# Spectral mixing after linear attention: the weights of two modes in one transfer, their products on row halves

## The chip, the cores and the metric

The kernel runs on one core of a Trainium2 chip. The metric is the device time of one execution in microseconds (us). The kernel before has a median of 425.22 us over four runs (425.04 to 426.35). One execution was profiled; its trace tells when each instruction of each engine ran and when each DMA packet moved.

The core's engines are TensorE (PE in the profile; its weight loads are the row PEld), VectorE (DVE), ScalarE (ACT), GpSimd (POOL) and SyncE (SP). GpSimd and SyncE issue the DMA transfers here, and 16 DMA engines carry them out.

## The reference

The computation has two parts. The first is a linear attention without softmax for 8 batches, 8 heads, 576 rows and a head width of 64:

```python
phi(x) = max(x, exp(x) - 1) + 1          # the ELU feature, plus one
kv  = einsum('bhsd,bhse->bhde', phi(k), v)
z   = sum over s of phi(k)
x   = einsum('bhsd,bhde->bhse', phi(q), kv) / (phi(q) . z + 1e-6)   # then heads side by side: 8 x 576 x 512
```

The second part mixes the first 64 frequencies ("modes") of x along the sequence, each with its own complex 512 x 512 matrix, and adds a channel product:

```python
X  = rfft(x, axis=1)[:, :64]
Yr = Xr @ w_r[m] - Xi @ w_i[m]           # per mode m
Yi = Xr @ w_i[m] + Xi @ w_r[m]
u  = x + irfft(Y, n=576)
out = u + max(u @ w_ch, 0)
```

The weights `w_r` and `w_i` are 64 matrices each of 512 x 512 in 32-bit floats: 134 MB in all, read once. q, k and v are 9.4 MB each, and the output is 9.4 MB.

## The kernel before

**Loads.** Everything large comes through GpSimd's DMA queue, because it is cast on the way: q, k and v to 16-bit floats, the weights to bfloat16. `load(b)` (line 159) brings q, k and v of a batch; a partition holds runs of 9 rows of 64 numbers. q of the first batch comes uncast through SyncE. `w_load(kk, half, ...)` (line 103) brings half a mode: `half` 0 is `w_r[kk]`, 1 is `w_i[kk]`. A tile `w` is 128 partitions by 8 rows by 512 columns. Partition 2p holds rows 8p to 8p+7 of `w_r`, partition 2p+1 the same rows of `w_i`. So a transfer writes every second partition, 64 runs of 16 KB read and 8 KB written. There are four tiles in `wpool` (`W_KEEP`) and six more in `wpre` (`W_PRE`), the latter only until the first ten modes are done. During the attention stage `w_next()` issues single halves between the loads of batches. Later `w_get(kk)` issues a mode's two halves where the program wants a free tile, and GpSimd waits there until TensorE has finished the product that last read this tile. The last half of mode 63 is cut into four pieces (`PIECES`), so that work on it can begin early.

Each GpSimd transfer also tells its landing on one of eight semaphores in turn, and an issue waits until the transfer eight places before it has landed.

**Attention stage.** For each batch: `exps` (ScalarE) and `features` (VectorE) form phi; `turn_q` transposes phi(q) on TensorE and ScalarE copies the result; `sum_kv` sums phi(k) times v; `form_x` divides. `transform` multiplies x with the DFT matrix (`fwd_sb`), and `place_x` spreads the spectrum over the partitions with 0/1 matrices so that partition 2p meets `w_r` and 2p+1 meets `w_i`, with Xi negated where needed. It takes four matmuls per batch and ends in `xt_c`, the stationary operand of all products. This stage's order is written out by hand: `pin` keeps an instruction's place in the program.

**Modes.** `mode_product(kk, ...)` (line 401) takes eight matmuls (line 409), each with 128 rows of contraction and at most 32 columns of `xt_c`; the four column groups of the array hold four of the eight at a time (`tile_position=(0, c)`). VectorE (even modes) or ScalarE (odd) evicts the result, four matmuls with `pick_sb` (line 423) add the four groups and transpose, and every eight modes VectorE copies the collected `yt`. For the first ten modes the instructions are not pinned.

Between a mode's product and its picks stand items from the list `work`, so many per mode as `per_slot` says. For modes 10 to 31 the items compute the attention rows again, in the output's layout (`attention_rows`). For modes 32 to 55 they are the fold stage: for each of 36 tiles of output rows `fold` adds the inverse DFT of the first 32 modes, `turn_x` transposes, `channel_product` multiplies with `w_ch`. For modes 56 to 60 they are `form_z`, `form_y` and `fold_lead`, which prepare modes 32 to 55. `keep_warm` puts extra matmuls without use into the stream; `FILL` says how many per mode.

**Tail.** `last_mode` (line 435) forms mode 63's result. Then the last eight modes are transposed and multiplied with `w_ch`, and `finish` adds everything for pairs of output tiles and stores them through SyncE.

## Time and profile before

| | before |
|---|---|
| median of four runs | 425.22 us |
| profiled execution, its own time | 425.11 us |
| its span (first to last instruction) | 423.3 us |
| TensorE busy | 277.4 us (66%) |
| VectorE busy | 216.2 us (51%) |
| ScalarE busy | 159.2 us (38%) |
| GpSimd busy | 89.5 us (21%) |
| moved by DMA | 93.12 MB written, 220 GB/s mean |
| median time from issue to landing, half a mode (512 KB) | 15.9 us (`w_r`), 17.8 us (`w_i`) |
| mean granted TensorE clock | 0.801 |

The span is cut in 40 slices on the page, where a digit is the busy share in tenths. "PEclk" is the granted TensorE clock as a share of full speed. "DMA" is the packets' recorded time as a share of 16 DMA engines; it can be over 1, since records of packets on one engine may overlap. Sizes and GB/s of a transfer count what is written; a cast load reads twice as much. The chain is followed back from the last instruction: at each step to what released it, or to the instruction before it on its engine.

### The profile page before, as it was taken

How to read it: one execution, taken by the hardware profiler on the slowest of the kernel's cores; microseconds unless marked ns; L12 is line 12 of the kernel's file. 1: busy time of each engine (PE TensorE's matmuls, PEld its weight loads, DVE VectorE, ACT ScalarE, POOL GpSimd, SP SyncE). 2: the span in 40 equal slices, each digit the busy share in tenths (PEclk: the TensorE clock that was granted, in tenths of full speed). 3: DMA queues.
4: the chain of work that ended last, by engine and by line, in shares of the span. 5: the costliest groups of instructions: out<-in, count | busy, mean ns of one | idle time of the engine just before them, and what ended most of it. 6: DMA issues, size and time to landing. Idle time of an engine off the chain costs nothing.

```text
span 423.3 us, 6741 instructions
## 1 busy us (share of the span) xinstructions
PE 277.4 (66%) x2762; PEld 143.6 (34%) x2762; DVE 216.2 (51%) x444; ACT 159.2 (38%) x253; POOL 89.5 (21%) x161
## 2 busy tenths in 40 slices
PE   1358677788248543344433488788777879899992
PEld 0246455565112221111211233343333324374420
DVE  4599688894302463433634443444343434522794
ACT  4688578844121100000000144443433335231782
POOL 4222124222220321212221111211111222120000
PEclk9999688889955555555555578988999999999997
DMA  9999999999999999999999999999999999997697
GB/s 213 207 208 209 209 209 210 217 212 212 221 213 217 216 211 217 216 211 215 218 211 216 216 212 214 218 211 215 218 212 214 218 213 215 216 213 159 236 403 304
DMA packets 27550, 93.12 MB, mean 220 GB/s; under 512 B 3072, under 2 KB 15744, under 8 KB 19264
## 3 DMA queue, kind: packets, MB, share of 16 engines
q0 software_dynamic: 23264, 81.48, 96.1%
q1 hardware_dynamic: 4256, 11.22, 7.2%
q8 instruction: 21, 0.34, 0.3%
q14 instruction: 9, 0.07, 0.0%
HBM read 163.93 MB, written 9.44 MB: 410 GB/s over the span
## 4 chain that ended last, share of the span: by engine, by line
DMA 74%; PE 12%; ACT 3%; issue 3%; DVE 3%; POOL 3%; DVEq 0%; POOLq 0%; ACTq 0%
DMA w<-in_moe_w_i_dram 63%; DMA k<-in_k_dram 7%; DMA pick_sb<-row_pick 4%; PE P L409 3%; PE acc L684 3%; PE acc L723 2%; POOL w L109 2%; ACT ke L191 2%; DVE x L278 1%; ACT qe L191 1%; PE kvp L240 0%; PE qTp L220 0%; ACT qT L227 0%; PE eps L623 0%; POOL k L173 0%
## 5 line engine op out<-in xcount | busy, mean ns | idle before, releaser
L409 PE MATMUL P<-w,xt_c 128*32 128x512 bf16 (+1 forms) x504 | 58.2, 537 | 77.7 <-DMA w<-in_moe_w_i_dram 73.7
L109 POOL DMA_DIRECT2D w<-in_moe_w_r_dram x64 | 33.7, 526 | 216.8 <-PE P L409 193.6
L417 ACT CAST ys<-P 128x512 f16<-128x512 f32 x31 | 18.2, 586 | 125.5 <-PE P L409 121.2
L415 DVE CAST ys<-P 128x512 f16<-128x512 f32 x32 | 22.1, 692 | 73.9 <-PE P L409 59.6
L409 PEld LDWEIGHTS <-xt_c 128*32 128x32 bf16 (+1 forms) x504 | 15.9, 159 | 88.1 <-DMA w<-in_moe_w_i_dram 63.7
L623 PE MATMUL eps<-wch,xTw 128*128 128x512 f16 x144 | 40.8, 411 | 0.0
L109 POOL DMA_DIRECT2D w<-in_moe_w_i_dram x67 | 36.3, 541 | 21.1 <-DMA w<-in_moe_w_i_dram 13.6
L604 DVE TENSOR_TENSOR x_main<-ya,x_main 128x512 f32<-128x512 f32 x32 | 22.0, 691 | 33.0 <-PE ya L600 33.0
L145 PEld LDWEIGHTS <-qT 64*128 64x128 f16 (+1 forms) x640 | 21.1, 125 | 51.1 <-issue 38.5
L631 ACT CAST E<-eps 128x512 f16<-128x512 f32 (+1 forms) x40 | 21.2, 540 | 31.6 <-PE eps L623 31.5
L145 PE MATMUL num<-kv,qT 64*128 64x65 f16 (+1 forms) x320 | 13.7, 212 | 22.9 <-ACT kv L251 11.3
L606 ACT CAST x16w<-x_main 128x512 f16<-128x512 f32 x32 | 19.8, 618 | 23.5 <-DVE x_main L604 17.4
L278 DVE TENSOR_TENSOR x<-num,rd 128x512 f16<-128x512 f32 x32 | 22.1, 692 | 1.1
L220 PE MATMUL qTp<-id,qe 128*128 128x128 f16 x144 | 15.8, 298 | 10.1 <-DVE qe L204 9.5
L191 ACT ACTIVATE qe<-q 128x1152 f16<-128x1152 f16 (+1 forms) x16 | 17.9, 1157 | 9.4 <-DMA q<-in_q_dram 9.4
L423 PE MATMUL yt<-pick_sb,ys 128*128 128x16 f16 x252 | 16.2, 175 | 8.0 <-DVE ys L415 3.1
L423 PEld LDWEIGHTS <-ys 128*128 128x128 f16 x252 | 12.0, 102 | 23.5 <-DVE ys L415 7.8
L191 ACT ACTIVATE ke<-k 128x1152 f16<-128x1152 f16 x16 | 17.7, 1152 | 4.9 <-DMA k<-in_k_dram 3.6
L733 ACT ACTIVATE acc<-acc 128x512 f32<-128x512 f32 x34 | 18.1, 581 | 2.3 <-PE acc L684 1.0
L573 DVE TENSOR_TENSOR x_main<-nw,rd 128x256 f32<-128x256 f32 x32 | 11.5, 416 | 14.0 <-PE nw L145 14.0
L623 PEld LDWEIGHTS <-xTw 128*128 128x128 f16 x144 | 13.2, 104 | 13.3 <-issue 5.6
L220 PEld LDWEIGHTS <-qe 128*128 128x128 f16 x144 | 13.6, 139 | 11.1 <-DVE qe L204 9.9
(108 smaller groups left out, 458.9 us busy)
## 6 DMA issues: line engine op xcount, KB each, us to landing
w<-in_moe_w_r_dram POOLq DMA_DIRECT2D x64, 512.0 KB, 15.9
w<-in_moe_w_i_dram POOLq DMA_DIRECT2D x63, 512.0 KB, 17.8
out_dram<-x_main SPq DMA_DIRECT2D x11, 512.0 KB, 3.7
k<-in_k_dram POOLq DMA_DIRECT2D x8, 576.0 KB, 12.9
v<-in_v_dram POOLq DMA_DIRECT2D x8, 576.0 KB, 14.9
q<-in_q_dram POOLq DMA_DIRECT2D x7, 576.0 KB, 13.0
out_dram<-x_main SPq DMA_DIRECT2D x6, 256.0 KB, 3.4
q<-in_q_dram SPq DMA_DIRECT2D x2, 576.0 KB, 4.5
```

What stands on the lines that cost most here:

```text
L109: nc.gpsimd.dma_start(out=w_in[kk][half::2, dcs], in_=rows_of[:, dcs, :])
L145: mm = nc.tensor.matmul(num[hpo][orow, c0 : c0 + 65], qT[rows, hpp, h2, cols], kv_sb[rows, hpp, h2, :])
L191: pin(nc.scalar.activation(out=ev[:, c], in_=heads(nm, b, c), func=AF.Exp))
L220: nc.tensor.transpose(qT_ps[:, j].rearrange("p t r -> p (t r)"), phi["q", b][:, hpp, j].rearrange("p o d -> p (o d)"), id16,)
L278: nc.vector.tensor_tensor(out=dst.rearrange("p (o c d) -> p o c d", o=2, c=4), in0=nv[:, :, :, 0:64], in1=rden.unsqueeze(3).broadcast_to([ ...
L409: nc.tensor.matmul(P[c : c + n, :], xt_cols(dc, kk, n), w[:, dc, :], start=(dc < NDC), stop=(dc >= NDC), tile_position=(0, c), skip_group_ ...
L415: fixed(nc.vector.tensor_copy(out=st, in_=P))
L423: nc.tensor.matmul(yt_ps[:, ec, kk % 8, :], st[:, ec * 128 : ec * 128 + 128], pick_sb)
L604: pin(nc.vector.tensor_tensor(out=x, in0=acc, in1=x, op=ALU.add))
L606: pin(nc.scalar.copy(out=x16w[t], in_=x))
L623: nc.tensor.matmul(e_ps, xT[:, c, :], wch16[:, c, :], start=(c == 0), stop=(c == NDC - 1))
L631: pin(nc.scalar.copy(out=dst, in_=e_ps[:, cols]))
```

## The change

The weights are loaded by pairs of modes. A tile `w` now has 16 rows of 512 columns per partition and holds two modes: partitions 0 to 63 the even mode of pair p, partitions 64 to 127 the odd one, in both `w_r` on even and `w_i` on odd partitions. One transfer brings `w_r` (or `w_i`) of both modes, as 64 runs of 32 KB read and 16 KB written. There are two tiles of double size in `wpool` and three in `wpre`. The last pair keeps transfers of half a mode, in the old layout, with the same pieces at the end.

A product has 16 matmuls of 64 rows per mode, and those of the two modes of a pair alternate between the row halves (`mode_pair`). Both are evicted, then items of `work`, then the picks of both, then more items, then fillers. All pairs are pinned. `place_x` puts the two modes' spectra on the two partition halves, with 24 matmuls per batch, and the last pair's in the old layout. The columns of the DFT matrix are sorted by even and odd modes for this.

q of batches 1 to 7 is read in runs of 18 rows (4608 bytes) instead of 9, and `turn_q` writes with that stride. The items of `work` are dealt anew over pairs (`share`): attention rows over pairs 5 to 14, with the formation of the row sets (`row_sets`, `row_set`), which stood ahead of the loop, put in after eight of them; the fold stage from the end of pair 15 to that of pair 26; the form stage from the end of pair 27 to that of pair 29. There are 24 fillers instead of 64.

```diff
-    fwd = np.concatenate([np.cos(ang), -np.sin(ang)], axis=2)
+    by_parity = np.concatenate([m[0::2], m[1::2]])
+    fwd = np.concatenate([np.cos(ang)[:, :, by_parity], -np.sin(ang)[:, :, by_parity]], axis=2)
...
-    NDW = 2 * NDC
-    XDC = 2 * B * NM
+    NDW = 4 * NDC
+    NDL = NDW // 2
+    NMP = NM // 2
+    XDC = 2 * B * NMP
...
-        c0 = dc * XDC + kk
-        return xt_c[:, c0 : c0 + (n - 1) * NM + 1 : NM]
+        if kk // 2 == LAST:
+            part, dc = slice(0, 128), (dc // NDC * 2 + kk % 2) * NDC + dc % NDC
+        else:
+            part = HALVES[kk % 2]
+        c0 = dc * XDC + kk // 2
+        return xt_c[part, c0 : c0 + (n - 1) * NMP + 1 : NMP]
...
-    W_KEEP = 4
+    W_KEEP = 2
+    pin = tc.keep_in_program_order
     PIECES = (slice(0, 4), slice(4, 6), slice(6, 7), slice(7, 8))
-
-    def w_load(kk: int, half: int, pool, tag: str, bufs: int):
+    HALVES = [slice(0, 64), slice(64, 128)]
+
+    LAST = NM // 2 - 1
+
+    def w_load(p: int, half: int, pool, tag: str, bufs: int):
         if half == 0:
-            w_in[kk] = pool.tile([128, NDW, D], BF16, tag=tag, bufs=bufs, name=f"w{kk}")
-        rows_of = (moe_w_r, moe_w_i)[half][kk].rearrange("(p dc) e -> p dc e", dc=NDW)
-        for dcs in PIECES if (kk, half) == (NM - 1, 1) else (slice(0, NDW),):
-            tc.keep_in_program_order(
-                nc.gpsimd.dma_start(out=w_in[kk][half::2, dcs], in_=rows_of[:, dcs, :])
-            )
+            w_in[p] = pool.tile([128, NDW, D], BF16, tag=tag, bufs=bufs, name=f"w{p}")
+        two = (moe_w_r, moe_w_i)[half][2 * p : 2 * p + 2]
+        pin(
+            nc.gpsimd.dma_start(
+                out=w_in[p][half::2], in_=two.rearrange("g (r dc) e -> (g r) dc e", dc=NDW)
+            )
+        )
+
+    def w_load_last(pool, tag: str, bufs: int):
+        w_in[LAST] = pool.tile([128, NDW, D], BF16, tag=tag, bufs=bufs, name=f"w{LAST}")
+        for g in range(2):
+            for half in range(2):
+                rows_in = (moe_w_r, moe_w_i)[half][NM - 2 + g].rearrange("(p dc) e -> p dc e", dc=NDL)
+                for dcs in PIECES if (g, half) == (1, 1) else (slice(0, NDL),):
+                    dst = w_in[LAST][half::2, g * NDL + dcs.start : g * NDL + dcs.stop]
+                    pin(nc.gpsimd.dma_start(out=dst, in_=rows_in[:, dcs, :]))
 
     w_in: dict[int, object] = {}
 
 
-    W_PRE = 6
+    W_PRE = 3
...
-                "(hp r j) d -> r hp (j d)", r=128, j=NJ
+                "(hp r j) d -> r hp (j d)", r=128, j=2 * NJ if nm == "q" else NJ
...
-                    pin(nc.sync.dma_start(out=t, in_=rows_in[:, c::2, :]))
+                    pin(nc.sync.dma_start(out=t, in_=rows_in[:, :, c * NJ * Dh : (c + 1) * NJ * Dh]))
...
-            t = sA.tile([128, NHP, NJ * Dh], F16, tag=f"{nm}16", bufs=2, name=f"{nm}16_{b}")
+            shape = [128, 2, 2 * NJ * Dh] if nm == "q" else [128, NHP, NJ * Dh]
+            t = sA.tile(shape, F16, tag=f"{nm}16", bufs=2, name=f"{nm}16_{b}")
...
-    def turn_q(b, hpp):
-        qT = q_view(qT_all[b])
-        qT_ps = psA.tile([128, NJ, 2, NP], F16, tag="big", bufs=3, name=f"qTp{b}_{hpp}")
+    def turn_q(b, c):
+        qT = qT_all[b].rearrange("p (x j) -> p x j", j=2 * NJ)
+        qT_ps = psA.tile([128, NJ, 128], F16, tag="big", bufs=3, name=f"qTp{b}_{c}")
         for j in range(NJ):
             pin(
                 nc.tensor.transpose(
-                    qT_ps[:, j].rearrange("p t r -> p (t r)"),
-                    phi["q", b][:, hpp, j].rearrange("p o d -> p (o d)"),
+                    qT_ps[:, j],
+                    phi["q", b][:, c, j].rearrange("p o d -> p (o d)"),
                     id16,
                 )
             )
         pin(
             nc.scalar.copy(
-                out=qT[:, hpp].rearrange("p t (r j) -> p t r j", j=NJ),
-                in_=qT_ps.rearrange("p j t r -> p t r j"),
+                out=qT[:, :, c * NJ : (c + 1) * NJ], in_=qT_ps.rearrange("p j x -> p x j")
             )
         )
 
...
-    place = sA.tile([128, 2, 2, 128], BF16, name="place")
+    place = sA.tile([128, 4, 66], BF16, name="place")
+    place_l = sA.tile([128, 2, 130], BF16, name="place_l")
     nc.vector.memset(place, 0.0)
+    nc.vector.memset(place_l, 0.0)
 
     def make_place():
+        for i in range(4):
+            pin(nc.vector.tensor_copy(out=place[:, i, 1:65:2], in_=id16[:, i::4]))
         for i in range(2):
-            for o in range(2):
-                pin(nc.vector.tensor_copy(out=place[:, i, o, o::2], in_=id16[:, i::2]))
+            pin(nc.vector.tensor_copy(out=place_l[:, i, 1:129:2], in_=id16[:, i::2]))
 
     xsp = {}
+    PARTS = ((0, slice(1, 3)), (1, slice(0, 2)))
 
     def place_x(b):
 
-        x = xsp.pop(b)
-        ps = psA.tile([128, 2, 512], F32, tag="big", bufs=3, name=f"xp{b}")
+        x = xsp.pop(b).rearrange("p t c m -> p c t m")
+        ps = psA.tile([128, 4, NDC, 2, NMP], F32, tag="big", bufs=3, name=f"xp{b}")
+        for i in range(4):
+            for o, ts in PARTS:
+                for g in range(2):
+                    pin(
+                        nc.tensor.matmul(
+                            ps[HALVES[g], i, :, :, 0 : NMP - 1],
+                            place[:, i, 1 - o : 65 - o],
+                            x[:, :, ts, g * NMP : g * NMP + NMP - 1],
+                            start=(o == 0), stop=(o == 1), skip_group_check=True,
+                        )
+                    )
         for i in range(2):
-            for o, ts in ((0, slice(1, 3)), (1, slice(0, 2))):
-                pin(
-                    nc.tensor.matmul(
-                        ps[:, i], place[:, i, o, :], x[:, ts].rearrange("p t c m -> p (t c m)"),
-                        start=(o == 0), stop=(o == 1),
+            for g in range(2):
+                for o, ts in PARTS:
+                    pin(
+                        nc.tensor.matmul(
+                            ps[:, 2 * i + g, :, :, NMP - 1],
+                            place_l[:, i, 1 - o : 129 - o],
+                            x[:, :, ts, g * NMP + NMP - 1],
+                            start=(o == 0), stop=(o == 1), skip_group_check=True,
+                        )
                     )
-                )
...
+        h = NDW // 2
+        psf = ps.rearrange("p i c t m -> p (i c) t m")
+        pin(nc.vector.tensor_copy(out=xt_v[:, 0:h, :, b, :], in_=psf[:, 0:h]))
+        pin(nc.scalar.copy(out=xt_v[:, h:NDW, :, b, :], in_=psf[:, h:NDW]))
...
-            if b >= 1:
+            if b % 2 == 1:
...
-    def w_get(kk: int):
-        if kk not in w_in:
+    def w_get(p: int):
+        if p not in w_in and p == LAST:
+            w_load_last(wpool, "w", W_KEEP)
+        elif p not in w_in:
             for half in range(2):
-                w_load(kk, half, wpool, "w", W_KEEP)
-        return w_in.pop(kk)
+                w_load(p, half, wpool, "w", W_KEEP)
+        return w_in[p]
 
...
+    slots: dict = {}
+
+    def work_slot(p: int, name: str):
+        for _ in range(slots.get((p, name), 0)):
+            if work:
+                work.pop(0)()
+
+    def product(P, kk: int, w, dc: int):
+        last = kk // 2 == LAST
+        n_dc = NDL if last else NDW
+        c = dc % NDC * 32
+        n = 32 if dc < NDC else 2 * B
+        rows = slice(0, 128) if last else HALVES[kk % 2]
+        pin(
+            nc.tensor.matmul(
+                P[c : c + n, :], xt_cols(dc, kk, n), w[rows, dc, :],
+                start=(dc < NDC), stop=(dc >= n_dc - NDC), tile_position=(rows.start, c),
+                skip_group_check=True,
+            )
+        )
+
+    def evacuate(kk: int, P):
+        st = ystage.tile([128, D], F16, tag="ystage", bufs=2, name=f"ys{kk}")
         if kk % 2 == 0:
-            fixed(nc.vector.tensor_copy(out=st, in_=P))
+            pin(nc.vector.tensor_copy(out=st, in_=P))
         else:
-            fixed(nc.scalar.copy(out=st, in_=P))
-        work_slot(kk, 0)
-        work_slot(kk, 1)
-        keep_warm(fill[0])
+            pin(nc.scalar.copy(out=st, in_=P))
+        return st
+
+    def picks(kk: int, st):
         for ec in range(NDC):
-            fixed(
+            pin(
                 nc.tensor.matmul(
                     yt_ps[:, ec, kk % 8, :], st[:, ec * 128 : ec * 128 + 128], pick_sb
                 )
             )
...
+
+    def mode_pair(p: int):
+        nonlocal yt_ps
+        w = w_get(p)
+        kks = (2 * p, 2 * p + 1)
+        if p % 4 == 0:
+            yt_ps = psW.tile([128, NDC, 8, 2 * B], F32, tag="yt", bufs=1, name=f"yt{p // 4}")
+        Ps = [psW.tile([128, D], F32, tag="P", bufs=2, name=f"P{kk}") for kk in kks]
+        for dc in range(NDW):
+            for P, kk in zip(Ps, kks):
+                product(P, kk, w, dc)
+        sts = [evacuate(kk, P) for P, kk in zip(Ps, kks)]
+        work_slot(p, "mid")
+        for kk, st in zip(kks, sts):
+            picks(kk, st)
+        if p % 4 == 3:
+            if kks[1] < NF:
+                pin(nc.vector.tensor_copy(out=YE_T[:, :, kks[1] - 7 : kks[1] + 1, :], in_=yt_ps))
+            else:
+                g = (kks[1] - NF) // NL + 1
+                pin(nc.vector.tensor_copy(out=YL[:, :, :, g, :], in_=mode_rows(yt_ps)))
+        work_slot(p, "end")
+        keep_warm(FILL.get(p, 0))
+
+    def last_pair():
+        w = w_get(LAST)
+        kk = NM - 2
+        P = psW.tile([128, D], F32, tag="P", bufs=2, name=f"P{kk}")
+        for dc in range(NDL):
+            product(P, kk, w, dc)
+        st = evacuate(kk, P)
+        keep_warm(4)
+        picks(kk, st)
+        pin(nc.vector.tensor_copy(out=Y8[:, :, 0 : NL - 1, :], in_=yt_ps[:, :, 0 : NL - 1, :]))
+        keep_warm(6)
         kk = NM - 1
-        w = w_get(kk)
-        y_last = ps.tile([128, NDC, 2 * B], F32, tag="P", bufs=2, name="y_last")
-        for dc in range(NDW):
+        y_last = psW.tile([128, NDC, 2 * B], F32, tag="P", bufs=2, name="y_last")
+        for dc in range(NDL):
             for ec in range(NDC):
                 pin(
                     nc.tensor.matmul(
-                        y_last[:, ec, :], w[:, dc, ec * 128 : ec * 128 + 128], xt_cols(dc, kk, 2 * B),
-                        start=(dc == 0 and ec == 0), stop=(dc == NDW - 1), skip_group_check=True,
+                        y_last[:, ec, :], w[:, NDL + dc, ec * 128 : ec * 128 + 128],
+                        xt_cols(dc, kk, 2 * B),
+                        start=(dc == 0 and ec == 0), stop=(dc == NDL - 1), skip_group_check=True,
                     )
                 )
         nc.vector.tensor_copy(out=Y8[:, :, NL - 1, :], in_=y_last)
...
+    FILL = {**{p: 1 for p in range(20, 27)}, 27: 1, 28: 1, 29: 2, 30: 3}
...
+    for p in range(n_early):
+        mode_pair(p)
...
+    sel = sW.tile([128, 1 + N_LEAD, 128], F16, tag="rows", bufs=1, name="row_sel")
+
+    def row_sets():
+        pin(nc.vector.memset(sel, 0.0))
...
+    def row_set(i: int):
+        dst = ([inv2_sb] + lead_sb)[i]
         for cols in (slice(0, 512), slice(512, S)):
             r_ps = bank(f"rows{i}_{cols.start}")[:, 0 : cols.stop - cols.start]
-            nc.tensor.matmul(r_ps, sel[:, i, :], inv_sb[:, cols])
-            nc.scalar.copy(out=dst[:, cols], in_=r_ps)
+            pin(nc.tensor.matmul(r_ps, sel[:, i, :], inv_sb[:, cols]))
+            pin(nc.scalar.copy(out=dst[:, cols], in_=r_ps))
...
+    first_fold, first_form, n_form_p = NF // 2 - 1, NE // 2 - 1, 3
+    fold_pairs = first_form - first_fold
+
...
+    share(
+        n_fold,
+        [((first_fold, "end"), 5)]
+        + [((p, h), 3) for p in range(first_fold + 1, first_form) for h in ("mid", "end")],
+    )
+    share(
+        n_form,
+        [((first_form, "end"), 6)]
+        + [((p, h), 4) for p in range(first_form + 1, first_form + n_form_p) for h in ("mid", "end")],
+    )
...
+    rows_work = [row_sets] + [lambda i=i: row_set(i) for i in range(1 + N_LEAD)]
+    work[:0] = [lambda t=t: attention_rows(t) for t in tiles[:8]] + rows_work + [
+        lambda t=t: attention_rows(t) for t in tiles[8:]
+    ]
+    share(
+        len(tiles) + len(rows_work),
+        [((p, h), 1) for p in range(n_early, first_fold) for h in ("mid", "end")],
+    )
+
+    for p in range(n_early, LAST):
+        if p == LAST - 1:
...
+            slots[p, "mid"] = slots[p, "end"] = N_PRE
...
+        mode_pair(p)
+    last_pair()
+
+
+    last = sW.tile([128, 2, D], F16, tag="rows", bufs=1, name="last")
```

## The prediction

> **What bounds the kernel now.** I read the page's head and its slices first, then the DMA queues, then the stage table, then the chain that ended last, then single rows of TensorE.
>
> ```profile
> span 423.3 us, 6741 instructions
> PE 277.4 (66%) x2762; PEld 143.6 (34%) x2762; DVE 216.2 (51%) x444; ACT 159.2 (38%) x253; POOL 89.5 (21%) x161
> ...
> PEclk9999688889955555555555578988999999999997
> DMA  9999999999999999999999999999999999997697
> ...
> q0 software_dynamic: 23264, 81.48, 96.1%
> ```
>
> No compute engine is near full; the DMA row is at 9 in all but two slices. GpSimd's queue (q0) alone has packet time for 96.1% of the span, that is 407 us, though its loads run only from 5.5 to 391.4 us (first packet; last landing). So packets overlap each other, and most of a packet's recorded fixed time is hidden already. The stage table (columns: stretch, its length, then busy time and count of each engine, granted clock, DMA share, GB/s) shows the same:
>
> ```profile
> 24.00:40.00 16.00, 11.82 (x148) 9.50 (x149) 15.16 (x33) 13.18 (x15) 4.04 (x6) 1.00 1.19 210
> 160.00:200.00 40.00, 15.83 (x212) 7.19 (x216) 14.95 (x43) 2.34 (x4) 8.46 (x16) 0.50 1.04 215
> 260.00:290.00 30.00, 23.64 (x166) 10.31 (x164) 12.76 (x25) 12.49 (x24) 7.11 (x14) 0.90 1.03 214
> 390.00:423.30 33.30, 24.70 (x160) 8.91 (x160) 22.99 (x24) 19.73 (x38) 0.56 (x1) 0.93 0.80 301
> ```
>
> The share is 1.19 where packets are short (q, k, v) and 1.03 to 1.04 with weights, at nearly the same GB/s. The chain in order of time (start, us, what):
>
> ```profile
> 250.17 17.83 DMA w<-in_moe_w_i_dram
> 268.05 0.71 PE P L409 x7
> 269.56 17.99 DMA w<-in_moe_w_i_dram
> 287.60 0.72 PE P L409 x6
> 289.12 17.98 DMA w<-in_moe_w_i_dram
> ```
>
> Landings at 268.00, 287.55 and 307.10: 19.55 us for four modes, 4.89 per mode, whatever TensorE does between. A load waits 18 us because some 13 to 15 us of other loads stand ahead of it. Only an empty queue, or fewer bytes or less overhead in it, moves the last landing. Behind that lies a tail of 423.3 - 391.4 = 31.9 us, paced by VectorE (busy 23.0 us of 33.3).
>
> Now TensorE, where the clock is 0.50:
>
> ```profile
> 150.60 1.11 PE L409 MATMUL P<-w,xt_c 128*32 128x512 bf16 x8 [1.66 <-DMA w<-in_moe_w_i_dram]
> 151.65 0.63 PE L145 MATMUL nw<-kv,qT 64*128 64x65 f16 x16
> 152.51 0.28 PE L423 MATMUL yt<-pick_sb,ys 128*128 128x16 f16 x4 [0.23 <-DVE ys L415]
> 155.49 1.10 PE L409 MATMUL P<-w,xt_c 128*32 128x512 bf16 x8 [2.70 <-DMA w<-in_moe_w_i_dram]
> 156.52 0.41 PE L145 MATMUL nw<-kv,qT 64*128 64x65 f16 x8
> ...
> 245.26 0.61 PE L613 MATMUL xTp<-id,x16w 128*128 128x128 f16 x4
> 245.66 1.91 PE L623 MATMUL eps<-wch,xTw 128*128 128x512 f16 x4
> ...
> 249.50 1.03 PE L623 MATMUL eps<-wch,xTw 128*128 128x512 f16 x4
> ```
>
> A product is eight matmuls in two rounds of four column groups: 1.11 us; a record of one round alone took 0.65, so a further round costs 0.46. The 64-row matmuls of L145 alternate row halves: 16 take 0.63, 8 take 0.41, so 27.5 ns each. The last three lines are the fold stage, before and after the clock rose to 1.00 at 247.8.
>
> **Part 1: fewer packets and transfers.** A packet of 1152 B (written) is recorded with 107.2 ns, one of 8192 B with 625.2: 73.6 ns per 1000 B. A q, k or v transfer (32 packets per engine) so needs 32 x 1152 B = 2.71 us and lands every 2.845; a half of a mode (4 packets) needs 2.411 and lands every 2.443. The residues, 0.13 and 0.032 us, give (0.13 - 0.032) / 28 = 3.5 ns per packet and 0.018 us per transfer. The 31 first pairs take 62 transfers instead of 124, and 16 KB packets instead of 8 KB ones: per engine 4 x 62 = 248 packets fewer, 0.87 us, and 62 transfers fewer, 1.12 us. q of batches 1 to 7: 16 packets fewer per engine each, 7 x 16 x 3.5 ns = 0.39 us. Together 2.4 us. No row shows a 32 KB read; if it is cut in two packets, only 1.12 + 0.39 = 1.5 us go. At the other end all the weights' residue cannot go, so 2.4 is also the upper bound. I take 2.4, because the 16 KB read went as one packet.
>
> The Trainium skill, "DMA: Bandwidth & Descriptors", section "Anatomy of one DMA", fits 2.0 us plus bytes per transfer. By that 62 transfers fewer would give an estimated 124 us, if nothing overlapped; the row above has 0.032 us of everything that is not bytes, so the measurement decides.
>
> **Part 2: TensorE instructions.** The products become 1000 matmuls instead of 504, with 64 rows each. If both modes of a pair run side by side, as the halves in L145 do, a pair is four rounds: 0.65 + 3 x 0.46 = 2.03 us at half clock, against 2 x 1.11 = 2.22 before. If one follows the other it is eight rounds, 0.65 + 7 x 0.46 = 3.87. I take 2.03, by the L145 row, which is nearest. `place_x` goes from 4 to 24 matmuls per batch, half as wide or tiny: by 27.5 ns each between 0 and 0.6 us per batch, in a stage where loads stand 8.4 us or more ahead of each issue; nothing on the path. Three more instructions on VectorE (two copies of 0.24, one memset of 0.27), once, lie there too. The q copy, exps and features keep their sizes (1124 to 1157 ns). Row sets move from before the loop into the slots of pair 7: six matmuls (3.1 us) and eleven small VectorE instructions, where TensorE idles half the time. Fillers fall from 64 to 24.
>
> The Trainium skill, "TensorEngine Tiling (Array Packing)", section "Instruction Overhead", counts about 60 cycles of overhead per matmul, which speaks against the change. With the 2.4 GHz of its page "TensorE: Matmul & The Clock Gate" (introductory table) that is an estimated 12 us of TensorE for the 496 added ones. The products' rows above put them beside the transfers, and L145 shows starts 27.5 ns apart, so the sum would not move by it unless a pair's slack were used up.
>
> More code is fetched: 1232 more instruction rows on TensorE, with 21 packets for the present 6741 instructions some 4 packets of 0.95 us on one engine each, 0.24 us over 16; up to 0.95 if they all fall on the slowest. I take 0.25.
>
> **Part 3: cover that shrinks.** Buffers hold the same bytes, but come free by pairs. In the steady state a new load was issued with 13.2 us of landings ahead (three modes less 1.45). Now it is one pair, 9.7 us, less 2.03 for the product and 0.32 to issue: 7.4 us. What does an empty queue need? The tail's GpSimd load was issued at 394.01 with its first packet at 395.98, and a landing is told 0.33 us after the last packet: 2.3 us. So 5 us of lateness are free. Places:
>
> - Pairs 1 to 5. `pick_sb` landed at 125.30, and is now 0.7 earlier, 124.6. Then picks, product, eviction, picks of each pair follow in a fixed order: 2.03 + 0.8 (product's end to pick, as at 151.7 to 152.5) + 0.3 = 3.13 us. Product 5 ends at 124.95 + 4 x 3.13 + 2.03 = 139.5; pair 7 is issued at 139.85. Pair 6 lands at 124.6 + 19.4 = 144.0: 4.15 us are left, 1.85 above the need. Price 0; this is the thinnest place.
> - Fold stage (end of pair 15 to 26). A tile (fold, transposition, channel product) takes about 2.8 us at half clock and 1.5 at full, by the starts of these rows; three tiles and one transposition of 0.6 per pair are 9.0 or 5.1 us, plus product 2.03 or 1.15 and picks 0.4. That is 6.7 of 9.7 us at full clock; an all-cold pair needs 11.4 and makes the next 1.7 late, where 5 are free. Price 0.
> - Pair 29's product waits for form work of pair 28: about 1.6 us late, price 0. The last pair keeps the old transfers, pieces and `y_last`, and the tail its order; 0.
>
> **Sum.** -2.4 + 0.25 = -2.15 us: span 421.15. The profiled execution took 425.11, 1.81 over its span and 0.11 under the median of 425.22. So 422.96 for an execution like it and 423.07 against the median; I say 423.0. A difference of 0.3%, 1.3 us, is about what a measurement can tell from no change.
>
> **Rivals.**
> - The 32 KB run goes as two packets: 425.2 - 1.5 + 0.25 = 424.0, within 0.3%. For it: no row with 32 KB. Against: a packet already equals the whole 16 KB run.
> - Slower: the two row halves don't run side by side with four column groups each. From 0.4 us more per pair on, pairs 1 to 5 (1.85 / 5) let the queue run dry; at the full 1.84 us, product 5 ends 9.2 us later, and pair 7 is issued at 149.05 with its first packet at 151.0, when data ended at 143.7: 7.3 us of empty queue, 423.0 + 7.3 = 430.3. With half the loss, 2.7 us: 425.7. For it: no row of before uses row halves and 32-column groups at once. Against: each of the two is seen to overlap on its own.
> - Fold or form stage late by more than 5 us in a pair, with the clock falling to 0.5 since fillers go: each microsecond beyond counts; three pairs with 1 to 2 us are 427 to 429. Against: a busy TensorE got 1.00 at 247.8 without fillers.
> - The stream gains, but the clock falls before `y_last`: 1.61 us of y_last and some 3 us behind it slow, 1 to 1.5 us given back: 424.3.
>
> **How the numbers follow.** Forecast 0.61, two packets 0.07, halves one after another 0.12 (a third with so small a loss that it ends near 426, the rest to 430.3), late fold or form 0.11, cold end 0.09. Faster than 423.9: the forecast and a little of the second, 0.62. Within 0.3%: 0.06 of the second, 0.04 of the third, 0.06 of the cold end, 0.16. Slower than 426.5: 0.08 of the third, the late stages' 0.11 and 0.03 where a cold end goes with them, 0.22. The range starts at 421.8 (both bounds, a tail 1 us shorter by the slots' new order) and reaches to 428.5, which leaves out the worst of the stalls, about 0.1.
>
> **What would show it.** Right: packets of 16 KB, one per run; landings of a pair every 9.70 us instead of 9.77 from 160 to 370 us; the DMA row at 9; products of 32 matmuls in about 2.0 us at clock 0.50; last landing near 389.2 and a tail of 31.9. Wrong: packets of 8 KB; a landing interval near 140 to 155 us well over 5 us; products of 3.9 us; a chain that goes through folds instead of weights; a clock of 0.5 at the end.

## The result, and the profile after

| | before | after |
|---|---|---|
| median of all timed runs (55 and 34) | 425.21 us | 424.98 us |
| profiled execution, its own time | 425.11 us | 425.54 us |
| its span | 423.3 us | 423.7 us |
| last landing of weights | 391.39 us | 390.97 us |
| from there to the end (tail) | 31.9 us | 32.8 us |
| mean granted TensorE clock | 0.801 | 0.750 |

After to before, mean against mean, is 0.9977, with a 95% interval of 0.9969 to 0.9985: 1.0 us faster (0.6 to 1.3), where 2.2 were forecast (423.0). That lies within the 0.3% to which the prediction gave 0.16. Repeated runs of one kernel fall in two groups (before 425.0 to 425.6 and, 20 of 55, 426.2 to 428.1; after 423.5 to 424.0 and, 20 of 34, 424.9 to 425.6), so that the medians differ by only 0.2 us where the means differ by 1.0, and the profiled run of before is of its faster group, that of after of its slower one.

The page of after, its head, slices and DMA queues:

```profile
span 423.7 us, 7890 instructions
PE 283.2 (67%) x3378; PEld 152.2 (36%) x3378; DVE 215.5 (51%) x447; ACT 161.6 (38%) x253; POOL 56.6 (13%) x99
...
PEclk9999978898555555555555587889698896579998
DMA  9999999999999999999999999999999999987697
...
q0 software_dynamic: 16512, 81.47, 93.9%
...
q8 instruction: 26, 0.43, 0.4%
```

Its stage table (stretch, length, busy time and count of each engine, clock, DMA share, GB/s):

```profile
160.00:200.00 40.00, 17.79 (x308) 8.92 (x305) 17.04 (x52) 3.71 (x9) 4.23 (x8) 0.50 1.02 216
260.00:290.00 30.00, 24.48 (x226) 11.25 (x224) 13.85 (x27) 13.15 (x24) 3.17 (x6) 0.89 1.01 215
390.00:423.70 33.70, 25.12 (x166) 9.07 (x163) 23.45 (x25) 19.73 (x38) 0.57 (x1) 0.95 0.78 297
```

q0 has 6752 packets fewer, and its share fell from 96.1 to 93.9% at the same bytes. In the slices, compare the clock: before it stood at 9 from the 29th digit on; now there is a second valley (6, 5, 7) late in the modes, and the DMA row leaves 9 one slice earlier. q8 carries code: 26 packets against 21 before. In the stage table the share is down to 1.02 and 1.01 at much the same GB/s. The chain in order of time shows the steady part:

```profile
174.41 1.94 PE P L442 x25
176.35 0.35 PE nw L165 x8
...
176.72 0.52 POOL w L119
177.23 16.55 DMA w<-in_moe_w_i_dram
...
193.82 1.94 PE P L442 x20
```

Products start 19.41 us apart, here for two pairs (the chain skips every second one): 9.705 us per pair against 9.77 before. A product of 32 matmuls takes 1.94 us at half clock. Pair 30 landed at 379.27, mode 61 of before at 381.49: at that point the stream was 2.22 us ahead. Twelve microseconds later, at the last landing, it was 0.42 ahead, and the tail gave 0.8 back. So in this run the forecast gain existed and was lost behind 379 us. The late part of TensorE in after (start, us, engine, line, what; lines in between are left out):

```profile
371.36 1.98 PE L698 MATMUL z<-wch,YL 128*64 128x512 f16 x8
375.87 1.10 PE L442 MATMUL P<-w,xt_c 64*32 64x512 bf16 x32
383.92 1.10 PE L442 MATMUL P<-w,xt_c 64*32 64x512 bf16 x32
388.08 0.67 PE L442 MATMUL P<-w,xt_c 128*32 128x512 bf16 x8
390.95 1.07 PE L504 MATMUL y_last<-xt_c,w 128*128 128x16 bf16 x32
```

`y_last` in the kernel before, waiting for its weights:

```profile
390.11 1.61 PE L444 MATMUL y_last<-xt_c,w 128*128 128x16 bf16 x32 [0.19 <-DMA w<-in_moe_w_i_dram]
```

And GpSimd's issues in after, with the idle time before them in brackets:

```profile
362.79 0.54 POOL L119 DMA_DIRECT2D w<-in_moe_w_i_dram  x1
377.34 0.52 POOL L131 DMA_DIRECT2D w<-in_moe_w_r_dram  x1 [14.01 <-PE P L442]
```

Pair 29's product began at 375.87, 6.3 us after its weights (369.57). GpSimd waited 14.01 us for it and issued the last pair's loads with 1.92 us of landings ahead. The landings that followed, with their distance to the one before (from the trace's issues and times to landing; 2.44 is the distance in an undisturbed stream):

```
379.27  w_i of pair 30
382.44  +3.17   w_r of mode 62   (late issue: 0.73 over)
384.86  +2.42   w_i of mode 62
388.57  +3.71   w_r of mode 63   (1.27 over; issued with 6.47 us ahead)
390.97          last piece of w_i of mode 63
```

The second jump is not explained by a late issue. A code packet of q8 started at 386.4 us; runs below show what it did.

### The profile page after: what moved, and what is told of

The parts are those of the page before. It is cut to its first block, busy times and chain, and to the rows that moved or that the text cites. A ratio compares the mean times of both kernels' runs of the same rounds, so it can differ in the third digit from the quotient of the medians.

```text
span 423.7 us, 7890 instructions
## 1 busy us (share of the span) xinstructions
PE 283.2 (67%) x3378; PEld 152.2 (36%) x3378; DVE 215.5 (51%) x447; ACT 161.6 (38%) x253; POOL 56.6 (13%) x99
## 3 DMA queue, kind: packets, MB, share of 16 engines
q0 software_dynamic: 16512, 81.47, 93.9%
## 4 chain that ended last, share of the span: by engine, by line
DMA 63%; PE 23%; DVE 4%; ACT 3%; issue 3%; POOL 2%; DVEq 0%; POOLq 0%; ACTq 0%
DMA w<-in_moe_w_i_dram 47%; PE P L442 8%; DMA pick_sb<-row_pick 8%; DMA k<-in_k_dram 7%; PE acc L735 3%; PE z L698 2%; PE acc L774 2%; ACT ke L213 2%; POOL w L119 1%; PE zl L425 1%; DVE ys L452 1%; PE yp L711 1%; PE yt L460 1%; DVE x L299 1%; ACT qT L249 1%
## 5 line engine op out<-in xcount | busy, mean ns | idle before, releaser
L442 PE MATMUL P<-w,xt_c 64*32 64x512 bf16 (+2 forms) x1000 | 53.2, 558 | 61.5 <-DMA w<-in_moe_w_i_dram 60.1
L119 POOL DMA_DIRECT2D w<-in_moe_w_r_dram x31 | 16.5, 533 | 245.2 <-PE P L442 141.0
L442 PEld LDWEIGHTS <-xt_c 64*32 64x32 bf16 (+2 forms) x1000 | 17.1, 128 | 80.0 <-DMA w<-in_moe_w_i_dram 42.8
L676 PE MATMUL eps<-wch,xTw 128*128 128x512 f16 x144 | 43.2, 430 | 0.0
L165 PEld LDWEIGHTS <-qT 64*128 64x128 f16 (+1 forms) x640 | 23.3, 124 | 49.1 <-issue 28.1
L165 PE MATMUL nw<-kv,qT 64*128 64x65 f16 (+1 forms) x320 | 19.0, 240 | 9.5 <-DVE x_tail L620 4.3
L460 PE MATMUL yt<-pick_sb,ys 128*128 128x16 f16 x252 | 11.8, 174 | 14.3 <-DMA pick_sb<-row_pick 7.6
L249 ACT COPY qT<-qTp 128x1152 f16<-128x1152 f16 x16 | 19.6, 1290 | 0.5 <-PE qTp L242 0.2
L460 PEld LDWEIGHTS <-ys 128*128 128x128 f16 x252 | 9.8, 103 | 24.6 <-DVE ys L452 15.3
L119 POOL DMA_DIRECT2D w<-in_moe_w_i_dram x31 | 16.9, 544 | 4.6 <-DMA q<-in_q_dram 2.3
```

The lines of the kernel that those rows point to most:

```text
L119: nc.gpsimd.dma_start(out=w_in[p][half::2], in_=two.rearrange("g (r dc) e -> (g r) dc e", dc=NDW))
L165: mm = nc.tensor.matmul(num[hpo][orow, c0 : c0 + 65], qT[rows, hpp, h2, cols], kv_sb[rows, hpp, h2, :])
L249: nc.scalar.copy(out=qT[:, :, c * NJ : (c + 1) * NJ], in_=qT_ps.rearrange("p j x -> p x j"))
L442: nc.tensor.matmul(P[c : c + n, :], xt_cols(dc, kk, n), w[rows, dc, :], start=(dc < NDC), stop=(dc >= n_dc - NDC), tile_position=(rows.sta ...
L460: nc.tensor.matmul(yt_ps[:, ec, kk % 8, :], st[:, ec * 128 : ec * 128 + 128], pick_sb)
L676: nc.tensor.matmul(e_ps, xT[:, c, :], wch16[:, c, :], start=(c == 0), stop=(c == NDC - 1))
```

## Experiments

Theory at the start: the clock falls to 0.50 in pair 27, so the form stage is slow, pair 29's product late and the queue short. Rivals: the stream gains less than thought, or the form work dealt into pair 28 is too much at any clock.

**Is the stream's gain what it was taken for?** Each transfer of a pair cut in two:

```diff
-out=w_in[p][half::2], in_=two.rearrange("g (r dc) e -> (g r) dc e", dc=NDW)
+runs = two.rearrange("g (r dc) e -> (g r) dc e", dc=NDW)
+for dcs in (slice(0, NDL), slice(NDL, NDW)):
+    pin(nc.gpsimd.dma_start(out=w_in[p][half::2, dcs], in_=runs[:, dcs]))
```

> The changed kernel with each transfer of a pair cut in two of eight rows (124 transfers and 16 KB read per packet as in the kernel before; tiles, products and order stay). Prediction's price (0.018 us per transfer and 3.5 ns per packet): a pair lands every 9.77 us instead of 9.71, pair 30 lands at 381.2 to 381.4 us instead of 379.3, and since pair 29's product waits for the same chain of work after pair 28's landing, the end moves by the same: median 426.5 to 427. If the pair layout itself and not the longer runs made the stream faster, pair 30 still lands at 379.3 and the median stays at 425.0.

Pair 30 landed at 381.25 us, 1.98 later than in after; by 3.5 ns for 248 packets per engine and 0.018 us for 62 transfers it should be 1.98. Median 426.46 us (425.58 to 427.21), at the edge of the expected range; ratio to before 1.0014 (1.0001 to 1.0028).

Then the number of transfers left alone and only the runs halved, by a gap of two numbers in the tile's layout (28 of the 31 pairs):

```diff
-t = pool.tile([128, NDW, D], ...)
+t = pool.tile([128, 2, NDL * D + 2], ...)        # halves no longer adjacent
-in_=two.rearrange("g (r dc) e -> (g r) dc e", dc=NDW)
+in_=two.rearrange("g (r h dc) e -> (g r) h (dc e)", h=2, dc=NDL)
```

> The changed kernel with a gap of two numbers between the two halves of eight rows in the tiles of wpool (pairs 0, 1 and 5 to 30), so that the number of transfers stays and only the runs are cut to 16 KB read. Prediction's price of 3.5 ns per packet: a pair lands every 9.74 us instead of 9.71, that is 28 pairs x 8 packets x 3.5 ns = 0.8 us, pair 30 lands at about 380.0 us. If the whole residue is per transfer, 379.3; if it is all per packet, 381.1.

Pair 30 landed at 379.96, 0.69 later; 224 packets at 3.5 ns are 0.78. One run, 426.25 us. Both prices of the first part stand, each to about 0.2 us, since pair 30 of after itself landed 0.25 us earlier in two later profiles; the rival of a weaker stream falls.

**Does the clock make pair 29 late?** Fillers only:

```diff
-FILL = {**{p: 1 for p in range(20, 27)}, 27: 1, 28: 1, 29: 2, 30: 3}
+FILL = {**{p: 6 for p in range(20, 28)}, 28: 1, 29: 2, 30: 3}
```

> The changed kernel with six fillers per pair from pair 20 to 27 instead of one (the work, the transfers and their order unchanged). Clock theory: the form stage ran at a granted clock of 0.50 (351.8 to 375.7 us) because the idle time of each pair now lies in one piece and has one filler; with the fillers the clock stays at 1.00 from about 325 us on, pair 29's product starts at 369.5 to 371.5 us instead of 375.9, the last loads are issued with 5 us or more of landings ahead instead of 1.9, the last landing comes at about 389.1 instead of 391.0, and the median is 423.0 to 423.4 us. Block theory (two double tiles and form work dealt in big blocks make pair 29 late whatever the clock): the clock rises, but pair 29's product starts after 374 us, the queue still runs dry, and the median stays at 424.5 to 425.

Median 424.73 (423.44 to 426.16), ratio 0.9981 (0.9965 to 0.9998); 423.0 to 423.4 were expected. The profiled run took 423.46 us, one of the two fastest of twelve. The clock was not at 1.00 throughout, as the theory had it, but at 0.50 from 355.3 to 362.2 us; from there to the tail it stayed at 1.00. Its form work and product on TensorE:

```profile
369.68 1.09 PE L698 MATMUL z<-wch,YL 128*64 128x512 f16 x8
...
371.03 1.10 PE L442 MATMUL P<-w,xt_c 64*32 64x512 bf16 x32
```

GpSimd's issue after it:

```profile
372.49 0.52 POOL L131 DMA_DIRECT2D w<-in_moe_w_r_dram  x1 [8.76 <-PE P L442]
```

Eight `z` matmuls take 1.09 us instead of 1.98, the product starts 4.8 us earlier, the loads have 8.04 us ahead, and the tail is 31.9. So the clock decides whether pair 29 is late. But the last landing was 389.75, not 389.1: pair 30 landed 6.23 us after the landing before it instead of 4.85, of which the next landing gave 0.64 back. Something else cost 0.7 us, and the median moved little.

The other way to an early pair 29, less form work in pair 28 (weight 2 instead of 4 in its two slots, 6 in those of pair 29) and the fillers of after:

```diff
-+ [((p, h), 4) for p in range(first_form + 1, ...) for h in ("mid", "end")],
++ [((p, h), 2 if p == first_form + 1 else 6) for p in range(first_form + 1, ...) ...],
```

> The changed kernel with the form work dealt otherwise: weight 2 instead of 4 in the two slots of pair 28, 6 instead of 4 in those of pair 29; fillers as they are. Block theory: pair 29's product starts at 368 to 371 us, the queue never runs dry, last landing near 389.1, median 423.0 to 423.5. Clock theory: the loads are in time as well, but the form work at clock 0.50 is only pushed behind pair 29, so that pair 30's product and mode 62 come late, y_last starts at 391 us or later although its weights landed at 389, and the median is 424.3 to 425.2.

Pair 29's product began at 369.44 and the loads had 8.25 us ahead. The landing behind the issue was not late (381.58: +2.42), yet the median was 426.35 (424.49 to 427.01), ratio 1.0012 (0.9997 to 1.0026), more than either side had expected; the profiled run took 425.76. The work had only moved, as its rows on TensorE show:

```profile
384.30 1.10 PE L442 MATMUL P<-w,xt_c 64*32 64x512 bf16 x32
388.47 0.67 PE L442 MATMUL P<-w,xt_c 128*32 128x512 bf16 x8
391.34 1.07 PE L504 MATMUL y_last<-xt_c,w 128*128 128x16 bf16 x32
```

Pair 30's product stood 5.1 us behind its weights (379.16) and `y_last` ended 2.3 us after the last landing (before: 0.33). At half clock the form work is too long in either place. And a later landing was late by 1.2 us (388.83).

More fillers: sixteen in pair 27, eight of them inside its waits.

```diff
+FILL_27 = 4      # after pair 27's evictions, and again after its picks
-FILL = {**{p: 1 for p in range(20, 27)}, 27: 1, 28: 1, 29: 2, 30: 3}
+FILL = {**{p: 6 for p in range(20, 27)}, 27: 8, 28: 1, 29: 2, 30: 3}
```

> Theory (the gain is lost because the clock falls before the form stage): six fillers in pairs 20 to 26 and sixteen in pair 27, eight of them inside its waits for evictions and copies, keep the granted clock at 1.00 from 345 to 385 us more often than e1_fill's six did. Pair 29's product then begins at 369.5 to 371.5 us, the last loads are issued with over 6 us of landings ahead, the last landing is at 389.1 to 389.8, and the median is 423.0 to 423.7, with fewer than a third of the runs above 424.4 (e1_fill: 9 of 12). Rival (the size of the form stage's pieces is what is late, whatever the clock): no better than e1_fill, 424.7, or worse by the fillers' own time, up to 425.5.

The clock's part held: 1.00 from 340 to 370 and 0.98 to 380, product at 369.43, 9.03 us ahead. The median did not: 424.40 (424.10 to 425.39) where 423.0 to 423.7 were expected, ratio 0.9973 (0.9956 to 0.9989), the same as that of after. Six of twelve runs were above 424.4, and in e1_fill it was eight, not nine as the expectation says. The last landing was 389.75 as in e1_fill, again behind one landing 1.0 us late (379.92).

Whether fewer fillers alone bring the clock down, asked of the kernel before:

```diff
-FILL = {**{kk: (0, 3) for kk in range(44, 60)}, 60: (0, 1), 61: (2, 3), 62: (4, 6)}
+FILL = {**{kk: (0, kk % 2) for kk in range(40, 60)}, 60: (0, 1), 61: (1, 3), 62: (4, 6)}
```

> The kernel before, with its fillers cut from 64 to 24 and nothing else. Theory: fewer fillers let the clock fall to 0.50 somewhere between 295 and 375 us, but with four tiles of one mode each the form work holds up no load long enough: 13 us of landings lie ahead of an issue and 2.3 are needed, so the last landing stays at 391.4 (within 0.3) and the time at 425.2 to 425.9. Rival A (the fillers alone explain the loss): the same half clock costs here what it cost in the changed kernel, 1.5 to 2 us, 426.7 to 427.2. Rival B (the clock falls because of the longer pauses between pairs, not for want of fillers): the clock stays at 1.00 from 295 to 385 and the time at 425.2.

Two windows of after (columns as in the stage table; the clock is third from the end):

```profile
350.00:360.00 10.00, 6.34 (x69) 2.93 (x68) 4.29 (x7) 1.17 (x2) 1.05 (x2) 0.59 0.99 211
360.00:370.00 10.00, 9.48 (x66) 3.15 (x66) 3.19 (x5) 2.39 (x5) 1.06 (x2) 0.50 1.02 218
```

The first of them in the kernel before, with its 64 fillers:

```profile
350.00:360.00 10.00, 9.18 (x76) 4.63 (x75) 4.32 (x8) 4.91 (x9) 2.12 (x4) 1.00 1.04 216
```

Both in the kernel with fewer fillers:

```profile
350.00:360.00 10.00, 8.24 (x59) 4.26 (x60) 3.00 (x6) 3.89 (x7) 1.81 (x4) 0.83 1.03 215
360.00:370.00 10.00, 8.72 (x69) 3.85 (x65) 6.65 (x11) 3.51 (x6) 2.42 (x5) 1.00 1.03 215
```

With 25 fillers (the expectation counts 24) the clock of the kernel before halved for a third of one stretch and came back at once; the last landing was 391.13 and the profiled run took 424.98 us. The median was 425.83, the ratio 1.001 (0.9987 to 1.0033). In the profiled run the theory held, with a shorter fall than it had in mind, and few fillers alone did not keep the clock down as they did in after, where waits are gathered at pairs. But five of the ten runs took 426.4 to 428.1 us and none of these was profiled, so rival A is not ruled out for them.

**Two more profiles of after**, to see what makes its times differ:

> The changed kernel once more, for one more profile. Theory: its times fall in two groups (423.5 to 424.0 and 424.9 to 425.6) by whether the clock is kept. A run under 424.2 shows the clock at 1.00 for most of 345 to 376 us, pair 29's product begun before 373 and the last landing by 389.9; a run over 424.7 shows 0.50 there, the product at 375 to 377 and the last loads issued with under 2.3 us of landings ahead. Rival: the groups differ in the stream itself; pair 30 lands 1 to 1.5 us earlier in the faster one, at the same clock.

> The same kernel and the same expectation as for e0_again1: by the theory a run under 424.2 us has the clock at 1.00 for most of 345 to 376 us and pair 29's product begun before 373, one over 424.7 has 0.50 there and the product at 375 to 377; by the rival the landing of pair 30 differs by 1 to 1.5 us instead.

Both took 424.9 us and are alike: clock valley, product at 375.3, the first late landing only 0.30 over (2.74), the second 1.14 to 1.18 over (3.58, 3.62). So the theory held for a time over 424.7. A time under 424.2, as 14 of the 34 runs had, was not met, and what is different there stays open; the mean clock, on record for each run, does not tell (0.761 to 0.789 in those 14, 0.750 to 0.780 in the others). The jump behind the code packet near 386 was there again.

**The code packets.** I numbered q8's packets in the traces so far. From the 1st to the 26th of e1_fill TensorE ran 3178 matmuls, 127 for each on average. Behind the 17th a landing is late and stays 0.7 to 1.1 us behind, in the kernel before too (at 327.75 us); behind the 18th to 20th it is late by up to 0.9 us, of which all but 0.3 comes back with the next; behind the 25th 0.7 to 1.3 us stay again. Before has 20 packets ahead of its last landing, after 25. Theory: a packet of 0.94 us delays one DMA engine, and the 25th strikes the engine that is already the latest. First, fewer instructions: two batches' spectra placed by one set of matmuls.

```diff
-def place_x(b):                 # 24 matmuls per batch, 31 columns x 8
+def place_two(b):               # 24 matmuls per two batches, 31 columns x 16
...
-            if b > 1 and jj == 1:
-                place_x(b - 2)
+            if b > 1 and b % 2 == 1 and jj == 1:
+                place_two(b - 3)
```

> The changed kernel with the spectrum of two batches placed at once: 96 matmuls fewer on TensorE, nothing else. Theory (the 25th code packet delays the DMA engine that is already the latest): in the traces a code packet of 16 KB comes every 128 matmuls; the 17th and the 25th were followed by a landing 1.0 to 1.3 us late that was not made up, the others not. Here the 25th should come only after the last weights (after 391 us, against 386.4), the landing that took 3.71 us takes 2.4 to 2.6, the last landing is at 389.0 to 389.9 even if the clock falls and the last loads are issued late as before, and the median is 423.5 to 424.4. Rival (only the late issue costs): the last landing stays at 390.2 to 391.0 and the median at 424.7 to 425.2.

Median 423.37 (422.52 to 425.27), just under the expected range; ratio 0.9946 (0.9927 to 0.9965), against runs of before with a median of 426.17. Against the 425.21 of all its runs it is 1.8 us. The DMA queues from 384 to 389.5 us (packets, MB, share), of after:

```profile
q0 software_dynamic: 402, 1.03, 97.4%
q8 instruction: 1, 0.02, 1.1%
```

And of this kernel, with no packet of q8:

```profile
q0 software_dynamic: 361, 0.72, 69.8%
```

The 25th packet came at 390.7 us. The landing behind 386 took 2.44 us instead of 3.71, and the last one was 389.56, although the clock fell here too (0.65 and 0.67 in the two windows from 350 to 370), pair 29's product began only at 373.79 and the loads had 3.63 us ahead (0.63 lost there, +3.07).

Next, both cures:

```diff
 # place_two as above, FILL_27 as in e6_fill27
+FILL_27 = 4
-FILL = {**{p: 1 for p in range(20, 27)}, 27: 1, 28: 1, 29: 2, 30: 3}
+FILL = {25: 2, 26: 6, 27: 8, 28: 1, 29: 2, 30: 3}
```

> The same, with 34 fillers in place of 24 (two after pair 25, six after 26, sixteen in pair 27, the last pairs as in the changed kernel). Theory: both losses go. Clock at 1.00 for most of 345 to 385 us, pair 29's product begun by 372, the last loads issued with over 6 us of landings ahead, no code packet from 377 to 389, last landing at 388.3 to 389.1, and a median of 422.4 to 423.4. Rival (code packets do not matter, or the later code packet moves to another place among the last loads): the last landing is at 389.7 as in e1_fill and e6_fill27, median 423.4 to 424.7.

Its products on TensorE at the end, with the idle time before them:

```profile
379.20 1.11 PE L451 MATMUL P<-w,xt_c 64*32 64x512 bf16 x32 [1.47 <-DMA w<-in_moe_w_i_dram]
384.03 0.66 PE L451 MATMUL P<-w,xt_c 128*32 128x512 bf16 x8 [0.59 <-DMA w<-in_moe_w_i_dram]
387.86 1.44 PE L515 MATMUL y_last<-xt_c,w 128*128 128x16 bf16 x32 [0.80 <-DMA w<-in_moe_w_i_dram]
```

Every product waits for its weights again, none of the last landings is late by more than 0.1 us, and the last is at 388.96: 2.43 us before that of the kernel before. Five of six runs took 423.2 to 423.5. The profiled one is the sixth, 424.86: the clock fell at 389 (0.66 from 389 to 394), and its tail was 34.0 us instead of 31.9. Median 423.38, ratio 0.9944 (0.9928 to 0.9960): the same as e10_lean, and its expected 422.4 to 423.4 just met. (It has 40 fillers; the expectation counts 34.) These two beat both kernels. The earlier last landing, 388.96 against 389.56 in e10_lean, shows in the profiles and not in the medians.

Last, the number against the place: 256 tiny matmuls, so that each late packet's number is two higher.

```diff
+if 6 <= p < 14:
+    for _ in range(32):
+        pin(nc.tensor.matmul(last_ps[0][:, 0:8], id16, wch16[:, 0, 0:8]))
```

> The changed kernel with 256 tiny matmuls more (8 columns each, 32 after each of pairs 6 to 13, where TensorE has time), so that each later code packet has a number two higher. Theory (the number decides): the 25th comes near 350 to 356 us and a landing behind it is 0.9 to 1.3 us late for good, so that pair 30 lands at 380.0 to 380.7 instead of 379.0 to 379.3; the packet near 386 is now the 27th and the landing behind it takes 2.4 to 2.6 us, not 3.7. The last landing stays within 0.5 of 390.6. Rival (what costs is a code packet among the last loads, whichever it is): pair 30 at 379.0 to 379.4 and again 3.6 us at the landing behind 386.

The 25th packet came at 354.0 and the landing behind it took 6.25 us (the next 4.20, so 0.8 stay); the 27th came at 386.8, and the landing behind it took 2.46, where after had 3.71. The 17th moved likewise: it came at 217.1 instead of 249.3, the landing behind it took 6.27 (the next 4.22), and the one behind the packet at 249.0 took 5.01 where after had 5.92. In this run the number decided, not the place. Pair 30 landed at 379.90, 0.1 short of the expected range. The last landing missed it by more: 392.02, since the landing after the late issue was 1.95 over (4.39) with 1.90 us ahead; after lost only 0.73 with 1.92, and what makes the difference stays open. One run, 426.09 us.

## Why the prediction was right or wrong

**Fewer packets and transfers: right, and so were both prices.** A 32 KB run went as one packet (16384 B written, 1229 ns). The forecast was 2.4 us, 2.15 net of code; measured 2.22 at pair 30 (2.45 in the two later profiles), and e2_cut and e5_runs16 gave back 1.98 and 0.69 when the parts were undone. The 0.39 for q was not measured alone. The rival of two packets fell.

**Products on row halves: right.** 1.94 to 1.95 us at half clock against 2.03 worked out, so both modes run side by side. The rival of halves one after another fell; the time of the 496 added matmuls stayed beside the transfers (1.94 of 9.7 us per pair), but not their code, as said below.

**Pairs 1 to 5: the price of 0 was right.** ScalarE's copy behind `turn_q`, kept at 1124 ns in the prediction, took 1290. `pick_sb` came at 125.99 instead of 124.6, pair 7 was issued at 140.91 instead of 139.85, with 4.30 us ahead (forecast 4.15), and the landing behind it took 4.93 us. The steady distance ahead was 7.3 to 7.4 (forecast 7.4).

**"Pair 29's product waits for form work of pair 28: about 1.6 us late, price 0" is the step that failed first.** It was 6.3 us late (6.1 in the later profiles). The prediction gives no working for the 1.6 and names no clock; e1_fill, at 1.00 from 362 us on, had 1.59, so the figure is one of full clock. The rival "Fold or form stage late by more than 5 us in a pair, with the clock falling to 0.5 since fillers go" described it, at 427 to 429 us, but had 0.11, because a busy TensorE got 1.00 without fillers at 247.8. That row shows how the clock rose there, not how it is kept; and in after it stayed at 0.50 until 375.7 though TensorE was busy for 9.48 of the 10 us from 360 to 370. What took it, in windows of 3.4 us of after (its changes of clock are whole multiples of 3.41 us apart):

```profile
344.90:348.30 3.40, 3.30 (x20) 1.32 (x18) 1.08 (x3) 1.94 (x4) 0.00 (x0) 1.00 1.02 217
348.30:351.75 3.45, 1.12 (x33) 0.63 (x32) 0.38 (x1) 0.72 (x2) 0.08 (x1) 1.00 0.94 199
351.75:355.20 3.45, 2.29 (x20) 1.41 (x22) 1.00 (x2) 0.30 (x1) 0.97 (x2) 0.51 1.02 218
```

TensorE was busy 1.12 of 3.45 us, waiting for weights before pair 27's product and for the eviction behind it, and the clock halved at 351.8. The longest idle piece was 1.88 us. The Trainium skill, "TensorE: Matmul & The Clock Gate", section "Why this matters for your kernels", asks for no idle gap over about 3 us between bursts; here a stretch with no such gap was enough, so the measurement decides. The other six falls of after between 245 and 352 us agree: TensorE was busy for 0.5 to 2.1 of the 3.41 us before each and had not been idle for 3 us at a stretch when the clock fell, while after other such windows, with 1.7 us of work and more, it was kept. So what counts looks like the work in such a window, but no exact limit comes out of these runs.

The price in the profiles: the first late landing, 0.73 us (0.30 in the later ones), and the tail. "the tail its order; 0" failed with it, for TensorE came to `y_last` with work left over: it ended 1.05 us after the last landing instead of 0.33, and the tail is 0.8 longer. The need of 2.3 us ahead of an issue does not decide what is lost: e2_cut had 2.85 and lost 0.06, e10_lean had 3.63 and lost 0.63, while 8 us and more (e1_fill, e3_deal, e6_fill27, e12_both) lost nothing.

**"More code is fetched ... I take 0.25" was the mis-sized term.** It spread 0.95 us per packet over 16 engines, and named 0.95 as the bound if all four fall on the slowest; four on one engine would be 3.8. Five more packets came ahead of the last landing, and one of them, the 25th, cost 1.27 us in the profiled run, up to 1.18 in the later profiles, 0.7 to 1.2 net in e1_fill, e3_deal and e6_fill27. Fewer instructions alone (e10_lean) brought the median from 424.98 to 423.37.

In the times it is this term that shows. The ratios to before are 0.9977 for after, 0.9981 and 0.9973 with the clock mended (e1_fill, e6_fill27), 0.9946 with fewer instructions (e10_lean) and 0.9944 with both (e12_both): the late form work is seen in the profiles, but mending it moved no ratio beyond its interval.

For the later profiles, which stand nearest to the median: 391.39 of before, less 2.45, plus 0.30, plus 1.18, less 0.17 in the other landings, is 390.25; with a tail of 32.9 it makes a span of 423.1. The forecast had 389.24 and 31.9. With both losses cured the last landing was 388.96, and the median 423.4, which is near the forecast of 423.0 for reasons that it had right; the changed kernel's own median never got there.

## What to carry to other kernels

Here a stream that was saturated to the end paid for TensorE's code in steps: in such a case count the code packets ahead of the last landing, and merge matmuls where that can be done. When tiles are made larger, waits gather as well, and a TensorE that had its idle time in many short pieces may fall to half clock just before the work that the next load waits for; look at busy time by windows of 3.4 us, not at fillers or averages. Take cover from the DMA engine that runs out first, not from the landing, which is the last engine's.

## What the runs showed that was not expected

- The 16 DMA engines are far out of step. In before, the 128 packets of 1024 B of the last two pieces started over 4.15 us (386.83 to 390.98). So a landing tells of the slowest engine, and faster ones run dry while microseconds of landings seem to be ahead: in after TensorE's product of pair 29 fell into 375.7 to 379.1 us, where the DMA share was 0.60. The Trainium skill, "DMA: Bandwidth & Descriptors", section "Why a DMA increments its semaphore by 16 and not by 1", says that the engines of a transfer finish independently and that the semaphore counts them; these rows agree.
- In after, 120 of those 128 packets had started by 389.33 us and the last eight, as many as one engine has, from 390.03 to 390.60, 0.08 us apart. The last of all came 1.27 us after the 120th; in e12_both, whose 25th packet came at 388.97, behind the weights' packets, 0.32, but in e10_lean, whose 25th came at 390.7, still 0.88. So a lag of this kind is not the work of that packet alone. That the packets of code strike one engine again with a period of eight is inferred from the 17th and the 25th; the trace doesn't name the engine of a packet.
- A lag of one engine can be made up (the 18th to 20th packet) or stay; which, I can't say beforehand.
